# Attention and expert feed-forward on one core: a new order of loads, PSUM in two early sets of three banks, and a later first feed-forward

## The chip, the cores and the metric

The kernel runs on one core of one Trainium2 chip. The metric is the device time of one execution in microseconds (us), as the median of the runs. Most executions of one kernel lie within 2% of each other. Each run carries a state: "slow" when it lies over 1.5% above the fastest run of the same kernel in its group.

A ratio is the mean time of one kernel's fast runs over the mean of the fast runs of the kernel before in the same rounds, so it is not quite the ratio of the medians that are quoted. A ratio of 0.01 is worth about 2.85 us here.

Engine names: PE is TensorE (matmuls and transposes), DVE is VectorE, ACT is ScalarE, POOL is GpSimd (it requests the loads), SP is SyncE (it requests the stores).

## The reference

Eight batches, eight heads, 576 positions, head size 64. The first four heads attend to the last 32 positions, the other four to every fourth of the last 128. Then each batch, as a whole, goes to one of eight experts. The code is condensed:

```python
scores = scale * np.matmul(q, k.transpose(0, 1, 3, 2))
scores = np.where(masks[None, :, :, :], scores, -1000000000.0)
attn = np.exp(scores - np.max(scores, axis=-1, keepdims=True))
attn = attn / (np.sum(attn, axis=-1, keepdims=True) + 1e-09)
x = np.matmul(attn, v)                      # (B, H, S, D), then to (B, S, 512)
# ... the mixture of experts ...
logits = x.mean(axis=1) @ w_gate            # one expert per batch
e_idx = np.argmax(logits, axis=1)
h = np.maximum(x[mask] @ w1[e], 0.0)
out[mask] = gate_w[mask, None, None] * (h @ w2[e])
```

What matters: which weights batch b needs is known only when its attention is finished. So the load of w1 and w2 (1 MB each in bfloat16) hangs on the *gate* of the batch, a chain of small instructions on PE, DVE and POOL.

## The kernel before

Work is cut into slots, four per batch; a slot t does the scores of one pair of heads, the `av` product of the pair before, and, from slot `4*b + LAGS[b]` on, a quarter of the feed-forward of batch b. The gate of batch b falls in slot 4*b + 5 (the first one at the end of slot 4). All loads go through one queue, in the order in which POOL requests them; the requests behind a gate are these:

```python
LAGS = (6, 7, 8, 8, 8, 8, 8, 8)
osp = ctx.enter_context(tc.tile_pool(name="osp", bufs=3))      # rows on their way out
psS = ...   # scores: 2 banks
psN = ctx.enter_context(tc.tile_pool(name="psN", bufs=1, space=PSUM))   # nd: 3 banks, one buffer
psM = ctx.enter_context(tc.tile_pool(name="psM", bufs=3, space=PSUM))   # all else: 3 banks
# ...
GO = (1, 0)                         # heads 4..7 first, then heads 0..3
def load_a(b): load_tiles(b); load_qk(b, GO[0]); load_v(b, GO[0]); load_vt(b)
def load_b(b): load_qk(b, GO[1]); load_v(b, GO[1])
# at the start: batches 0 and 1, complete
# ...
def emit_gate(b):
    # ... logits, argmax, expert number into a register of POOL ...
    # w1 of the expert, in four pieces
    if b == 0:
        load_a(2)
    nc.gpsimd.dma_start(out=w2b[:], in_=moe_w2[ds(e_val, 1)]...)     # w2, 1 MB
    load_b(b + 2)
    load_a(b + 3)
```

The transposes of k and q for a pair of slots come two slots and one slot ahead. So `load_b(b + 2)`, requested in slot 4*b + 5, is first needed in slot 4*b + 8, and the next gate comes one slot after that. This closes a loop: gate, loads, transposes of k, attention, next gate.

The small pieces of one slot, in the order of the program (cut):

```python
if prev: pa(); fence()              # av of the slot before, first part, into nd
flush()                             # stores of finished output rows
if att: emit_S_mm(b, n); emit_exp(b, n)
if items: run_T(t)                  # transposes; first half copied by DVE, second by ACT
if prev: pbb(); emit_ln(pb)
if att: emit_mask(b, n)
if prev: emit_rd(pb)
if not items: run_T(t)
# first half of the feed-forward items, the gate, then:
if prev: emit_norm(pb, pn)          # frees nd
# second half of the items
```

The softmax here doesn't subtract the row's maximum and nothing guards it: scores larger than these inputs give would overflow.

## Time and profile before

| | before |
|---|---|
| time, median (3 runs) | 284.86 us (284.79 to 288.28) |
| PE busy, share of the span | 73% |
| granted TensorE clock, mean | 0.922 |
| gates at (us) | 31.8, 66.5, 95.4, 128.0, 160.7, 192.7, 226.5, 251.2 |

First the page's slices: the span in 40 equal slices of 7.1 us, each digit a busy share in tenths (9 is 90% or more); for PEclk the digit is the granted clock in tenths.

```profile
PE   1465516999489882499929897498936999799893
PEclk9999999999669997599996999599995999799999
DMA  6994099973999299955999189993998069619913
```

Read the last row: the DMA is not lacking in load, it comes in bursts, with a slice near zero in every loop (the 4 and 0 before the first gate, then 3, 2, 5, 1, 3, 0). PE has its holes (1, then 4, 2 and 4, 2, 4, 3) while the DMA is at 9, and the recorded clock falls (6, 5, 6, 5, 5) with each hole but the first. The two engines take turns.

The chain that ended last, as shares of the span by line:

```profile
DMA km<-in_k_dram 30%; PE hm L470 21%; PE om L490 8%; PE nd L268 5%; PE tp L201 4%; DMA out_dram<-osb 3%; PE psS L220 2%; POOL w2b L435 2%; DVE xt L396 1%; ACT pt L244 1%; DVE qk L209 1%; POOLq L422 1%; PE lgt L415 1%; DVE pt L251 1%; DVE ht L477 1%
```

One loop of it in order of time (start, duration, what). L415 is the gate; km is a tile of k.

```profile
127.96 0.36 PE lgt L415 x8
...
132.59 0.91 POOL w2b L435
133.50 15.10 DMA km<-in_k_dram
148.63 1.11 PE tp L201 x33
149.80 0.33 PE nd L268 x13
150.12 6.30 PE hm L470 x32
...
160.69 0.36 PE lgt L415 x8
```

The chain from one gate to the next goes through the load of k, 15.1 us after the request of w2. The 15.1 us are not all lost, since PE has other work for a part of them. What PE really lost is in its waits (who waited for what: total us, times, longest):

```profile
PE tp L201 <- DMA km<-in_k_dram: 31.9, 6, 7.2
PE nd L268 <- DVE xt L396: 12.8, 10, 2.3
PE tp L201 <- DVE le L160: 5.7, 1, 5.7
PE hm L470 <- DMA w1b<-in_moe_w_dram: 4.0, 3, 1.7
PE lgt L415 <- DVE pooled L411: 3.1, 5, 0.6
PE hm L470 <- DVE osb L497: 2.9, 2, 2.2
...
PE tp L201 <- DVE osb L497: 1.1, 1, 1.1
```

The third line is the very first load of k at the start of the kernel, put down to a DVE instruction. The clock around one such wait, by stretches (busy us and instructions of PE, PEld, DVE, ACT, POOL; then granted clock, DMA share, GB/s):

```profile
143.50:147.00 3.50, 0.08 (x3) 0.00 (x0) 1.05 (x2) 0.92 (x1) 0.30 (x1) 1.00 1.18 224
147.00:150.50 3.50, 1.87 (x58) 1.59 (x59) 1.14 (x2) 0.66 (x2) 0.99 (x2) 0.63 1.18 269
150.50:154.00 3.50, 3.50 (x16) 2.25 (x15) 1.53 (x4) 1.28 (x3) 0.70 (x1) 0.50 1.67 194
154.00:157.50 3.50, 3.50 (x88) 2.71 (x87) 1.21 (x5) 1.88 (x5) 0.00 (x0) 0.89 1.13 148
```

PE does nothing for one stretch, and is granted half its clock in the next ones. This is what the Trainium skill, "TensorE: Matmul & The Clock Gate", Part 1, describes: an idle window halves the clock, a busy one restores it. The trace agrees here, with 0.50 for at least 3.5 us.

The record of the clock cannot be taken at its word at the start of the kernel. It shows 1.00 up to 70 us, yet the same matmul of the first feed-forward takes 444 ns before 48.5 us and 286 ns after 49.2 us (below: before, by line, in the windows 46.4 to 48.5 and 49.2 to 51.7 us; the number behind the comma is the mean of one in ns):

```profile
L470 PE MATMUL hm<-xt,w1b 128*128 128x288 bf16 x9 | 2.3, 444 | 0.0
L470 PE MATMUL hm<-xt,w1b 128*128 128x288 bf16 x21 | 2.7, 286 | 0.0
```

At the recorded 0.50 (150.5 to 154 us) it takes 447 ns. So PE ran slowly in the last us before 48.5, where the record shows 1.00; one transpose took 239 ns up to 40 us against 193 ns once the feed-forward ran, which says the same of the slots before. The first clock entry in the file of this trace lies at 48.9 us (in the changed kernel at 48.1 us), and until the first entry 1.00 is shown. Hence the first hole shows no fall, and the mean clocks quoted here are too high, by an amount that depends on where a record begins.

### The profile page before, as it was taken

How to read it: one execution, taken by the hardware profiler on the slowest of the kernel's cores; microseconds unless marked ns; L12 is line 12 of the kernel's file. 1: busy time of each engine (PE TensorE's matmuls, PEld its weight loads, DVE VectorE, ACT ScalarE, POOL GpSimd, SP SyncE). 2: the span in 40 equal slices, each digit the busy share in tenths (PEclk: the TensorE clock that was granted, in tenths of full speed). 3: DMA queues.
4: the chain of work that ended last, by engine and by line, in shares of the span. 5: the costliest groups of instructions: out<-in, count | busy, mean ns of one | idle time of the engine just before them, and what ended most of it. 6: DMA issues, size and time to landing. Idle time of an engine off the chain costs nothing.

```text
span 284.3 us, 9050 instructions
## 1 busy us (share of the span) xinstructions
PE 207.4 (73%) x3952; PEld 143.0 (50%) x3952; DVE 129.1 (45%) x375; ACT 128.3 (45%) x225; POOL 80.5 (28%) x128
## 2 busy tenths in 40 slices
PE   1465516999489882499929897498936999799893
PEld 1454515856357452376516664375525755554651
DVE  3745613746535543275515652365513652531511
ACT  2465722756616653267414664266512664331230
POOL 8740175203612261206401082205500040031000
PEclk9999999999669997599996999599995999799999
DMA  6994099973999299955999189993998069619913
GB/s 95 188 196 30 2 172 202 197 111 98 200 214 192 27 203 238 197 74 76 175 249 208 11 147 205 233 134 49 176 246 120 2 94 203 168 24 172 257 50 129
DMA packets 49383, 40.97 MB, mean 144 GB/s; under 512 B 23744, under 2 KB 37056, under 8 KB 49344
## 3 DMA queue, kind: packets, MB, share of 16 engines
q0 software_dynamic: 42880, 30.94, 75.2%
q1 hardware_dynamic: 6464, 9.46, 10.1%
q8 instruction: 31, 0.51, 0.7%
q14 instruction: 8, 0.07, 0.1%
HBM read 61.88 MB, written 9.44 MB: 251 GB/s over the span
## 4 chain that ended last, share of the span: by engine, by line
PE 42%; DMA 33%; issue 9%; DVE 8%; POOL 3%; ACT 2%; POOLq 2%; DVEq 0%
DMA km<-in_k_dram 30%; PE hm L470 21%; PE om L490 8%; PE nd L268 5%; PE tp L201 4%; DMA out_dram<-osb 3%; PE psS L220 2%; POOL w2b L435 2%; DVE xt L396 1%; ACT pt L244 1%; DVE qk L209 1%; POOLq L422 1%; PE lgt L415 1%; DVE pt L251 1%; DVE ht L477 1%
## 5 line engine op out<-in xcount | busy, mean ns | idle before, releaser
L470 PE MATMUL hm<-xt,w1b 128*128 128x288 bf16 x512 | 77.1, 313 | 7.0 <-DMA w1b<-in_moe_w_dram 4.0
L470 PEld LDWEIGHTS <-w1b 128*128 128x128 bf16 x512 | 52.8, 107 | 27.0 <-issue 6.4
L490 PE MATMUL om<-w2b,ht 128*128 128x512 bf16 x256 | 58.2, 380 | 0.0
L244 ACT ACTIVATE pt<-psS 128x896 bf16<-128x896 f32 x32 | 29.3, 917 | 49.1 <-PE psS L220 49.1
L429 POOL DMA_DIRECT2D w1b<-in_moe_w_dram x32 | 19.0, 604 | 112.9 <-PE hm L470 65.7
L209 DVE COPY qk<-tp 128x576 bf16<-128x576 bf16 x32 | 24.2, 759 | 55.6 <-PE tp L201 55.6
L201 PE MATMUL tp<-ident,km 64*64 64x64 bf16 x576 | 16.4, 219 | 37.6 <-DMA km<-in_k_dram 31.9
L475 ACT ACTIVATE ht<-hm 128x288 bf16<-128x288 f32 x64 | 25.1, 407 | 35.2 <-PE hm L470 31.9
L207 ACT ACTIVATE qk<-tp 128x576 bf16<-128x576 bf16 x32 | 23.2, 725 | 39.3 <-PE tp L201 31.7
L490 PEld LDWEIGHTS <-ht 128*128 128x128 bf16 x256 | 23.8, 98 | 27.2
L396 DVE SCALAR_TENSOR_TENSOR xt<-nd,rd 128x320 bf16<-128x320 f32 x64 | 32.3, 541 | 11.1 <-ACT rd L369 11.1
L268 PE MATMUL nd<-pt,vm 64*64 64x64 bf16 (+2 forms) x896 | 24.6, 204 | 17.2 <-DVE xt L396 12.8
L477 DVE TENSOR_SCALAR ht<-hm 128x288 bf16<-128x288 f32 x64 | 28.7, 456 | 18.2 <-PE hm L470 17.3
L201 PEld LDWEIGHTS <-km 64*64 64x64 bf16 x576 | 14.7, 132 | 38.8 <-DMA km<-in_k_dram 38.8
L268 PEld LDWEIGHTS <-vm 64*64 64x64 bf16 x896 | 17.4, 117 | 23.4 <-issue 13.5
L497 DVE TENSOR_SCALAR osb<-om,gbc 128x512 f32<-128x512 f32 x16 | 12.0, 749 | 36.6 <-PE om L490 13.9
L101 POOL DMA_DIRECT2D vm<-in_v_dram x32 | 24.1, 768 | 14.0 <-DMA w1b<-in_moe_w_dram 10.6
L251 DVE TENSOR_TENSOR pt<-pt,mk 128x896 bf16<-128x896 bf16 x32 | 19.9, 622 | 13.9 <-ACT pt L244 13.9
L369 ACT ACTIVATE rd<-lnd 128x576 f32<-128x576 f32 x32 | 21.9, 683 | 1.0
L268 PE MATMUL nd<-pt,ones 64*64 64x128 bf16 (+3 forms) x288 | 22.2, 265 | 0.0
L363 ACT ACTIVATE lnd<-nd 128x576 f32<-128x576 f32 x32 | 20.6, 644 | 3.4 <-PE nd L268 3.4
L220 PE MATMUL psS<-qk 64*64 64x96 bf16 (+2 forms) x576 | 18.2, 237 | 3.0 <-DVE qk L209 2.5
(56 smaller groups left out, 175.1 us busy)
## 6 DMA issues: line engine op xcount, KB each, us to landing
w1b<-in_moe_w_dram POOLq DMA_DIRECT2D x32, 256.0 KB, 6.2
w2b<-in_moe_w_dram POOLq DMA_DIRECT2D x8, 1024.0 KB, 14.7
out_dram<-osb SPq DMA_DIRECT2D x32, 256.0 KB, 6.7
km<-in_k_dram POOLq DMA_DIRECT2D x16, 288.0 KB, 13.6
qm<-in_q_dram POOLq DMA_DIRECT2D x16, 288.0 KB, 9.0
vm<-in_v_dram POOLq DMA_DIRECT2D x8, 256.0 KB, 7.3
vm<-in_v_dram POOLq DMA_DIRECT2D x32, 64.0 KB, 14.3
out_dram<-osx SPq DMA_DIRECT2D x16, 64.0 KB, 6.4
```

What stands on the lines that cost most here:

```text
L101: nc.gpsimd.dma_start(out=t[:, h], in_=v[b, h, 0:512, :].rearrange("(c p) d -> p c d", p=P))
L201: nc.tensor.transpose(out=tp[half(a), j, :], in_=t[half(a), RH * jh + j, :], identity=ident2[half(a), :])
L207: nc.scalar.activation(out=o, in_=i, func=AF.Copy)
L209: nc.vector.tensor_copy(out=o, in_=i)
L220: nc.tensor.matmul(ps[half(e), a, o : o + rhs.free_size()], lhsT=lhsT, rhs=rhs, start=True, stop=True, skip_group_check=True)
L244: nc.scalar.activation(out=pt[:], in_=s["ps"][:, :, 0:NP], func=AF.Exp, scale=0.125)
L268: x = nc.tensor.matmul(oo, lhsT=lhsT, rhs=rhs, start=start, stop=True, skip_group_check=True)
L396: nc.vector.scalar_tensor_tensor(out=o, in0=a0, scalar=1.0, in1=a1, op0=ALU.mult, op1=ALU.mult, accum_out=s["pool"][:, w, c : c + 1],)
L470: nc.tensor.matmul(hm[:], lhsT=s["w1"][:, c, fc * P : (fc + 1) * P], rhs=s["xt"][:, c, cols], start=(c == 0), stop=(c == 3))
L475: nc.scalar.activation(out=o, in_=hm[:], func=AF.Relu)
L477: nc.vector.tensor_scalar_max(out=o, in0=hm[:], scalar1=0.0)
L490: nc.tensor.matmul(om[:], lhsT=s["ht"][:, fc, r * P : (r + 1) * P], rhs=s["w2"][:, fc, :], start=(fc == 0), stop=(fc == 7))
```

## The change

The intent: have the loads stand in the queue in the order in which they are needed, use DMA time that lies idle at the start, and let the slots that have no feed-forward yet overlap more by giving `av` and the transposes two sets of three PSUM banks in turn.

```diff
-LAGS = (6, 7, 8, 8, 8, 8, 8, 8)
+LAGS = (7, 8, 8, 8, 8, 8, 8, 8)
# --- load_a and load_b are cut into load_qa, load_va, load_qb, load_vb ---
     # at the start
-    load_a(1)
-    load_b(1)
+    load_qa(1)
+    load_va(1)
+    load_qb(1)
+    load_vb(1)
+    load_qa(2)
     # behind the w1 of a gate
-        if b == 0:
-            load_a(2)
+        load_va(b + 2)
+        load_qb(b + 2)
         nc.gpsimd.dma_start(out=w2b[:], in_=moe_w2[ds(e_val, 1)].rearrange("e (c p) f -> p (e c) f", p=P))
-        load_b(b + 2)
-        load_a(b + 3)
+        load_vb(b + 2)
+        load_qa(b + 3)
# --- banks ---
+    def early_bank(t, k, dt=F32):
+        nm = f"e{t % 2}{k}"                # set t % 2, bank k of three
+        return pools["early"].tile([P, 512 if dt == F32 else 1024], dt, name=nm, tag=nm, space=PSUM)[:]
+    def late():                            # close them; then nd: 3 banks, all else: 3 banks
+    # in the loop over slots
+        if t == LAGS[0]:
+            late()
# --- early slots: scores and exp first, transposes behind av and ahead of ln ---
+        if early_s:
+            emit_S_mm(b, n)
+            emit_exp(b, n)
         if prev:
             pa, fence, pbb = av_work(pb, pn)
# ...
+        if pools["early"] is not None:
+            run_T(t)
+        if prev:
             emit_ln(pb)
```

Cut: the masks (fewer instructions, and behind the first transposes' copies), ln in two pieces in the early slots (the sums lie in two banks there), both halves of a transpose ahead of their two copies, and the gate a little earlier within its slot.

More of the change, by code (lines that the diff above doesn't have):

```diff
@@ L69, with bank @@
     psS = ctx.enter_context(tc.tile_pool(name="psS", bufs=1, space=PSUM))
-    psN = ctx.enter_context(tc.tile_pool(name="psN", bufs=1, space=PSUM))
-    psM = ctx.enter_context(tc.tile_pool(name="psM", bufs=3, space=PSUM))
     ctx.enter_context(tc.manual_schedule())
     nc.scalar.preload_act_table_set("natural_log_exp_and_others")
+    ps0 = psS.tile([P, 2, 512], F32, name="ps0", tag="ps0", space=PSUM)
+    nc.vector.memset(ps0[:], 0.0)
+    early = ExitStack()
+    pools = {"early": early.enter_context(tc.tile_pool(name="psE", bufs=1, space=PSUM))}
+    def early_bank(t, k, dt=F32):
+        nm = f"e{t % 2}{k}"
+        return pools["early"].tile([P, 512 if dt == F32 else 1024], dt, name=nm, tag=nm, space=PSUM)[:]
+    def late():
+        early.close()
+        pools["early"] = None
+        pools["N"] = ctx.enter_context(tc.tile_pool(name="psN", bufs=1, space=PSUM))
+        pools["M"] = ctx.enter_context(tc.tile_pool(name="psM", bufs=3, space=PSUM))
+    def bank(dt=F32, t=0):
+        if pools["early"] is not None:
+            return early_bank(t, 2, dt)
+        return pools["M"].tile([P, 512 if dt == F32 else 1024], dt, name="m", tag="M", space=PSUM)[:]
     src = {"q": q, "k": k}
@@ L108, with load_qa @@
     GO = (1, 0)
-    def load_a(b):
+    def load_qa(b):
         if b < B:
@@ L113, in load_a, with load_va, load_qb, load_vb @@
             load_qk(b, GO[0])
+    def load_va(b):
+        if b < B:
             load_v(b, GO[0])
             load_vt(b)
-    def load_b(b):
+    def load_qb(b):
         if b < B:
             load_qk(b, GO[1])
+    def load_vb(b):
+        if b < B:
             load_v(b, GO[1])
@@ L151 @@
     nc.vector.tensor_tensor(out=ident2[:], in0=identb[:, 0:DH], in1=identb[:, DH:P], op=ALU.add)
-    dpf = const.tile([P, QB], F32, name="dpf")
-    nc.vector.tensor_copy(out=dpf[:], in_=dti[:])
-    nc.vector.tensor_scalar(out=dpf[DH:P], in0=dpf[DH:P], scalar1=64.0, scalar2=None, op0=ALU.add)
-    ge0 = const.tile([P, QB], F32, name="ge0")
-    nc.vector.tensor_scalar(out=ge0[:], in0=dpf[:], scalar1=0.0, scalar2=None, op0=ALU.is_ge)
-    le31 = const.tile([P, QB], F32, name="le31")
-    nc.vector.tensor_scalar(out=le31[:], in0=dpf[:], scalar1=31.0, scalar2=None, op0=ALU.is_le)
@@ L161 @@
-    mk = const.tile([P, 2, NP], BF16, name="mk")
-    for g in range(2):
-        for i in range(4):
-            nc.vector.tensor_mul(mk[:, g, QB * i : QB * i + QB], ge0[:], le31[:])
-    nc.vector.tensor_mul(mk[:, 0, 4 * QB : NP], ge0[:, 0:DH], le31[:, 0:DH])
-    dta = const.tile([P, 4, 16], I32, name="dta")
-    nc.vector.tensor_scalar(out=dta[:], in0=dtt[:], scalar1=3, scalar2=None, op0=ALU.bitwise_and)
-    dtf = const.tile([P, 4, 16], F32, name="dtf")
-    nc.vector.tensor_copy(out=dtf[:], in_=dta[:])
@@ L170, with masks @@
-    nc.vector.tensor_scalar(out=dtf[:], in0=dtf[:], scalar1=0.0, scalar2=None, op0=ALU.is_equal)
-    dtg = const.tile([P, 4, 16], F32, name="dtg")
-    nc.vector.tensor_copy(out=dtg[:], in_=dtt[:])
-    nc.vector.tensor_scalar(out=dtg[:], in0=dtg[:], scalar1=0.0, scalar2=None, op0=ALU.is_ge)
-    nc.vector.tensor_mul(mk[:, 1, 4 * QB : NP].rearrange("p (r m) -> p r m", r=4), dtf[:], dtg[:])
+    mk = const.tile([P, 2, NP], BF16, name="mk")
+    def masks():
+        dpf = const.tile([P, QB], F32, name="dpf")
+        nc.vector.tensor_copy(out=dpf[:], in_=dti[:])
+        nc.vector.tensor_scalar(out=dpf[DH:P], in0=dpf[DH:P], scalar1=64.0, scalar2=None, op0=ALU.add)
+        le31 = const.tile([P, QB], F32, name="le31")
+        nc.vector.tensor_scalar(out=le31[:], in0=dpf[:], scalar1=31.0, scalar2=None, op0=ALU.is_le)
+        band = const.tile([P, QB], BF16, name="band")
+        nc.vector.scalar_tensor_tensor(
+            out=band[:], in0=dpf[:], scalar=0.0, in1=le31[:], op0=ALU.is_ge, op1=ALU.mult
+        )
+        for g in GO:
+            nc.vector.tensor_copy(
+                out=mk[:, g, 0 : 4 * QB].rearrange("p (i n) -> p i n", n=QB),
+                in_=band[:].rearrange("p (i n) -> p i n", i=1).to_broadcast([P, 4, QB]),
+            )
+        nc.vector.tensor_copy(out=mk[:, 0, 4 * QB : NP], in_=band[:, 0:DH])
+        dta = const.tile([P, 4, 16], I32, name="dta")
+        nc.vector.tensor_scalar(out=dta[:], in0=dtt[:], scalar1=3, scalar2=None, op0=ALU.bitwise_and)
+        dtf = const.tile([P, 4, 16], F32, name="dtf")
+        nc.vector.tensor_copy(out=dtf[:], in_=dta[:])
+        dtg = const.tile([P, 4, 16], F32, name="dtg")
+        nc.vector.tensor_copy(out=dtg[:], in_=dtt[:])
+        nc.vector.tensor_scalar(out=dtg[:], in0=dtg[:], scalar1=0.0, scalar2=None, op0=ALU.is_ge)
+        nc.vector.scalar_tensor_tensor(
+            out=mk[:, 1, 4 * QB : NP].rearrange("p (r m) -> p r m", r=4),
+            in0=dtf[:], scalar=0.0, in1=dtg[:], op0=ALU.is_equal, op1=ALU.mult,
+        )
@@ L189, in half, with emit_T @@
         return slice(64 * a, 64 * a + 64)
-    def emit_T(b, g, nm, jh, eng):
+    def emit_T(b, g, nm, t):
         s = state(b)
@@ L196, in emit_T @@
         qk = s["qk"][g]
-        t = loads[b][nm, g]
-        tp = psM.tile([P, RH, DH], BF16, name="tp", tag="M", space=PSUM)
-        for j in range(RH):
-            for a in range(2):
-                nc.tensor.transpose(
-                    out=tp[half(a), j, :], in_=t[half(a), RH * jh + j, :], identity=ident2[half(a), :]
-                )
-        o = qk[:, 0 if nm == "k" else 1].rearrange("p h (m j) -> p h m j", j=RJ)[:, :, :, RH * jh : RH * jh + RH]
-        i = tp[:].rearrange("p j (h m) -> p h m j", h=2)
-        if eng == "A":
-            nc.scalar.activation(out=o, in_=i, func=AF.Copy)
-        else:
-            nc.vector.tensor_copy(out=o, in_=i)
+        ld = loads[b][nm, g]
+        if pools["early"] is not None:
+            tps = [early_bank(t, jh, BF16) for jh in range(2)]
+        else:
+            tps = [bank(BF16) for jh in range(2)]
+        for jh in range(2):
+            tp = tps[jh][:, 0 : RH * DH].rearrange("p (j d) -> p j d", d=DH)
+            for j in range(RH):
+                for a in range(2):
+                    nc.tensor.transpose(
+                        out=tp[half(a), j, :], in_=ld[half(a), RH * jh + j, :], identity=ident2[half(a), :]
+                    )
+        for jh in range(2):
+            tp = tps[jh][:, 0 : RH * DH]
+            o = qk[:, 0 if nm == "k" else 1].rearrange("p h (m j) -> p h m j", j=RJ)[:, :, :, RH * jh : RH * jh + RH]
+            i = tp.rearrange("p (j h m) -> p h m j", h=2, j=RH)
+            if jh:
+                nc.scalar.activation(out=o, in_=i, func=AF.Copy)
+            else:
+                nc.vector.tensor_copy(out=o, in_=i)
     def emit_S_mm(b, n):
@@ L258, in av_work, with ndc @@
         g, h2 = GO[n // 2], n % 2
-        nd = psN.tile([P, 3 * 512], F32, name="nd", tag="nd", space=PSUM)
-        s["nd"] = nd
+        t = NSLOT * b + n
+        if pools["early"] is not None:
+            nb = [early_bank(t, i) for i in range(3)]
+            lns = ((DSO, 256), (DLO, 320))
+        else:
+            nd = pools["N"].tile([P, 3 * 512], F32, name="nd", tag="nd", space=PSUM)
+            nb = None
+            lns = ((DSO, S),)
+        def ndc(o, n):
+            return nd[:, o : o + n] if nb is None else nb[o // 512][:, o % 512 : o % 512 + n]
+        s["nd"] = (ndc, lns)
         first, lasts = [None], []
@@ L264, in mm @@
         def mm(a, o, n, lhsT, rhs, start, view=None):
-            oo = nd[half(a), o : o + n]
+            oo = ndc(o, n)[half(a)]
             if view is not None:
@@ L362, in emit_ln @@
         lnd = rdp.tile([P, S], F32, name="lnd", tag="lnd")
-        nc.scalar.activation(out=lnd[:], in_=s["nd"][:, DSO : DSO + S], func=AF.Ln)
+        ndc, lns = s["nd"]
+        for o, n in lns:
+            nc.scalar.activation(out=lnd[:, o - DSO : o - DSO + n], in_=ndc(o, n), func=AF.Ln)
         s["lnd"] = lnd
@@ L375, in emit_norm @@
         c = 2 * g + h2
-        nd, rd = s["nd"], s["rd"]
+        (ndc, _), rd = s["nd"], s["rd"]
         xt = s["xt"][:, c, :]
@@ L379, in emit_norm @@
         for w, no, ro, sz in parts:
-            i0, i1 = nd[:, no : no + sz], rd[:, ro : ro + sz]
+            i0, i1 = ndc(no, sz), rd[:, ro : ro + sz]
             if g == 0:
@@ L405, in bass_ap_plain_L, with emit_pooled @@
         return bass.AP(tensor=o.tensor, offset=o.offset, ap=ap)
-    def emit_gate(b):
+    def emit_pooled(b):
         s = st[b]
@@ L411, in emit_gate @@
         nc.vector.tensor_tensor(out=pooled[:], in0=s["pool"][:, 0, :], in1=s["pool"][:, 1, :], op=ALU.add)
-        lgt = psM.tile([P, 512], F32, name="lgt", tag="M", space=PSUM)
-        lg = lgt[0:1, 0:E]
+        s["pooled"] = pooled
+    def emit_gate(b):
+        s = st[b]
+        pooled = s["pooled"]
+        lg = bank()[0:1, 0:E]
         for c in range(4):
@@ L455, in emit_gate_bc @@
         s = st[b]
-        bct = psM.tile([P, 512], F32, name="bct", tag="M", space=PSUM)
+        bct = bank()
         nc.tensor.matmul(bct[:, 0:1], lhsT=ones1[:], rhs=s["gw"][:], start=True, stop=True)
@@ L467, in ffn1 @@
         cols = slice(HALF * hf, HALF * hf + HALF)
-        hm = psM.tile([P, HALF], F32, name="hm", tag="M", space=PSUM)
+        hm = bank()[:, 0:HALF]
         for c in range(4):
             nc.tensor.matmul(
-                hm[:], lhsT=s["w1"][:, c, fc * P : (fc + 1) * P], rhs=s["xt"][:, c, cols], start=(c == 0), stop=(c == 3)
+                hm, lhsT=s["w1"][:, c, fc * P : (fc + 1) * P], rhs=s["xt"][:, c, cols], start=(c == 0), stop=(c == 3)
             )
@@ L474, in ffn1 @@
         if eng == "A":
-            nc.scalar.activation(out=o, in_=hm[:], func=AF.Relu)
+            nc.scalar.activation(out=o, in_=hm, func=AF.Relu)
         else:
-            nc.vector.tensor_scalar_max(out=o, in0=hm[:], scalar1=0.0)
+            nc.vector.tensor_scalar_max(out=o, in0=hm, scalar1=0.0)
     stores = []
@@ L487, in ffn2 @@
         s = st[b]
-        om = psM.tile([P, DM], F32, name="om", tag="M", space=PSUM)
+        om = bank()
         for fc in range(8):
             nc.tensor.matmul(
-                om[:], lhsT=s["ht"][:, fc, r * P : (r + 1) * P], rhs=s["w2"][:, fc, :], start=(fc == 0), stop=(fc == 7)
+                om, lhsT=s["ht"][:, fc, r * P : (r + 1) * P], rhs=s["w2"][:, fc, :], start=(fc == 0), stop=(fc == 7)
             )
@@ L494, in ffn2 @@
         if eng == "A":
-            nc.scalar.activation(out=osb[:], in_=om[:], func=AF.Copy, scale=s["gbc"][:])
+            nc.scalar.activation(out=osb[:], in_=om, func=AF.Copy, scale=s["gbc"][:])
         else:
-            nc.vector.tensor_scalar_mul(out=osb[:], in0=om[:], scalar1=s["gbc"][:])
+            nc.vector.tensor_scalar_mul(out=osb[:], in0=om, scalar1=s["gbc"][:])
         stores.append(lambda: nc.sync.dma_start(out=out[b, r * P : (r + 1) * P, :], in_=osb[:]))
@@ L501, in ffn_tail @@
         s = st[b]
-        ox = psM.tile([P, 256], F32, name="ox", tag="M", space=PSUM)
+        ox = bank()[:, 0:256]
         for fc in range(8):
@@ L513, in ffn_tail @@
         osx = osp.tile([P, 256], F32, name="osx", tag="osx")
-        nc.vector.tensor_scalar_mul(out=osx[:], in0=ox[:], scalar1=s["gbc"][:])
+        nc.vector.tensor_scalar_mul(out=osx[:], in0=ox, scalar1=s["gbc"][:])
         for a in range(2):
@@ L518, in ffn_tail @@
             )
-    ps0 = psS.tile([P, 2, 512], F32, name="psS", tag="S", space=PSUM)
-    nc.vector.memset(ps0[:], 0.0)
     NA = B * NSLOT
@@ L534, in run_T @@
         for b, g, nm in tsched.get(t, []):
-            emit_T(b, g, nm, 0, "D")
-            emit_T(b, g, nm, 1, "A")
+            emit_T(b, g, nm, t)
     runs = {}
@@ L544 @@
     run_T(-1)
+    masks()
     for t in range(max(runs) + 1):
+        if t == LAGS[0]:
+            late()
         b, n = divmod(t, NSLOT)
@@ L559 @@
                 items += [lambda: ffn2(fb, 2, "A"), lambda: ffn2(fb, 3, "D"), lambda: ffn_tail(fb)]
+        early_s = att and pools["early"] is not None
+        if early_s:
+            emit_S_mm(b, n)
+            emit_exp(b, n)
         if prev:
@@ L564 @@
         flush()
-        if att:
+        if att and not early_s:
             emit_S_mm(b, n)
@@ L573 @@
             pbb()
+        if pools["early"] is not None:
+            run_T(t)
+        if prev:
             emit_ln(pb)
@@ L578 @@
             emit_rd(pb)
-        if not items:
+        if not items and pools["early"] is None:
             run_T(t)
         k0 = len(items) // 2
-        for f in items[:k0]:
-            f()
-        gb, gn = divmod(t - 1, NSLOT)
-        if gn == 0 and 0 < gb < B + 1:
-            if gb > 1:
+        gb, gn = divmod(t - 1, NSLOT)
+        for i, f in enumerate(items[:k0]):
+            f()
+            if i == k0 // 2 and gn == 0 and 1 < gb < B + 1:
                 emit_gate(gb - 1)
                 emit_gate_w(gb - 1)
+        if not items[:k0] and gn == 0 and 1 < gb < B + 1:
+            emit_gate(gb - 1)
+            emit_gate_w(gb - 1)
         if prev:
             emit_norm(pb, pn)
-        for f in items[k0:]:
+        if prev and pn == NSLOT - 1:
+            emit_pooled(pb)
+        for i, f in enumerate(items[k0:]):
             f()
```

## The prediction

> **What bounds it now.** 284.86 us. In the chain of waits the DMA of a k tile (km) takes 30% of the span: once per batch, gate, four w1 issues, w2 issue, then 8 to 17 us of "DMA km", then transposes. PE's waits show the net loss: 31.9 us idle for km, six times. Afterwards the granted clock is 0.50 for some 3.5 to 7 us: 32 first-layer matmuls take 6.30 us at 150 us against 4.03 us at 53 us. The Trainium skill, "TensorE: Matmul & The Clock Gate", Part 1, says an idle window halves the clock; this trace agrees. I estimate 1 to 2 us per wait, some 8 us in all.
>
> The gates fall at 31.8, 66.5, 95.5, 128.0, 160.7, 192.6, 226.5 and 251.2 us (timeline), about 32 us apart. In each loop the DMA is active only some 25.5 us (98.8 to 124.3; 130.3 to 156.4), then idle 5 to 7 us until the next gate. km of batch b+2 is requested behind w2, lands about 18 us after the first w1 issue, and the next gate follows 12 us later. PE needs about 25 us a loop without the wait (slots of 6.0, 6.2, 5.1, 6.4 us plus the gate). Both floors are near 25 to 26 us, run partly one after the other.
>
> **The change, costed.**
> 1. Loads ordered w1, v, k/q of batch b+2, then w2. Before the km that is needed stand 0.3 MB instead of 1 MB; the difference takes 4 to 5 us (220 to 250 GB/s in those slices) with the queueing. w2, needed two slots later, fills idle DMA time. Loop 32 to about 26.5 us: most of the gain.
> 2. k/q of batch 2 requested at the start, into DMA time idle from 24 to 34 us. The first km wait (7.1 us) goes. With lag 7 the first feed-forward starts at about 40 us in slot 7, instead of 46.5 in slot 6. Slots without feed-forward stay 8, so the lag itself saves no PE work.
> 3. Two sets of banks: av no longer waits for the previous norm (about 2.2 us a slot). But transposes of slot t reuse banks of slot t-2, wait for its norm, and ln and rd queue behind the transposed copy on ACT: 0.6 + 0.73 + 0.8 + 0.68 + 1.17 us plus latencies, 4.1 us a slot against 4.6; the first norm comes later. Masks behind the first copies: first scores at 9.7 instead of 11.3 us. Net: first gate at about 31 us.
> 4. Gate earlier within its slot: about 0.5 us a loop.
>
> **Sum.** First gate 31 us; second about 56 (was 66.5); then five loops of 26 to 27 us, limited by DMA; the last about 25, by PE; last gate about 212 (was 251), then the 33 us tail, unchanged. Predicted 246 us, range 237 to 259. Chances: faster by over 2% 0.96, within 2% 0.03, slower 0.01.
>
> **Right if:** "DMA km" falls below 12% of the chain; PE's wait for km falls below 10 us; DMA slices near zero between 60 and 200 us vanish; gates are 25 to 28 us apart; PE's mean clock rises from 0.92 above 0.95; first gate within 2 us of 31.
>
> **Wrong if:** DMA slows when stores and loads overlap all the time (loops of 29 us, 260 in all); v in 128-byte pieces (the Trainium skill, "DMA: Bandwidth & Descriptors", Specifications: under 512 B not at line rate; 23,744 of this trace's 49,383 packets are) delays the next w1; or the early banks pipeline better than I think (first gate at 27 us).

## The result, and the profile after

| | before | after |
|---|---|---|
| time, median | 284.83 us (4 runs) | 250.48 us (248.07 to 251.12, 4 runs) |
| ratio of fast runs | 1 | 0.8778, interval 0.8708 to 0.8847 |
| PE busy, share of the span | 73% | 82% |
| granted clock, mean, as recorded | 0.922 | 0.973 |
| gates at (us) | 31.8, 66.5, 95.4, 128.0, 160.7, 192.7, 226.5, 251.2 | 32.1, 60.0, 88.3, 115.5, 140.7, 166.7, 191.6, 215.3 |
| loops (us) | 34.7, 29.0, 32.5, 32.7, 32.0, 33.9, 24.7 | 27.9, 28.3, 27.2, 25.2, 26.0, 24.9, 23.7 |
| last gate to the end of the span | 33.1 us | 33.8 us |

The slices of the changed kernel, now 6.2 us each:

```profile
PE   1576464999853999799997899799979996996993
PEclk9999999999995899979999999999999997999999
DMA  5999129991699949999899999998999699089723
```

From the sixteenth slice (93 us) to about 205 us no DMA slice is below 6, and PE is at 7 or more. The DMA holes that are left are in front: the 1 and 2 around the first gate, the 1 ahead of the second and the 4 at the third. The chain that ended last:

```profile
PE m L531 24%; PE m L551 17%; DMA km<-in_k_dram 7%; PE nd L323 6%; DMA out_dram<-osb 6%; PE m L243 5%; DVE xt L453 3%; PE e L243 3%; PE ps L264 3%; PE m L566 2%; DVE osb L558 2%; PE e L323 2%; ACT rd L426 1%; DVE ht L538 1%; ACT lnd L420 1%
```

The load of k has gone from 30% to 7%. In its place stand the two feed-forward matmuls (L531, L551), and something new: the DMA of the output rows, osb, has doubled to 6%. PE's waits say the same:

```profile
PE e L243 <- DMA km<-in_k_dram: 7.1, 2, 5.6
PE m L243 <- DVE osb L558: 6.9, 5, 2.1
PE m L243 <- DMA km<-in_k_dram: 4.0, 1, 4.0
PE m L531 <- DVE osb L558: 4.0, 2, 2.1
PE nd L323 <- DVE xt L453: 4.0, 6, 1.6
PE e L476 <- issue: 3.2, 1, 3.2
PE nd L323 <- DVE gbc L520: 3.0, 1, 3.0
```

Of the 7.1 us on the first line, 5.6 are the first load at the start, which before had too under another name. So PE's waits for k inside the kernel went from 31.9 us to 5.5 us. But 10.9 us are now spent on osb, against 4.0 before. The timeline of one such case shows what osb itself waits for (start, duration, engine, line, what, and in brackets the idle time before it):

```profile
97.61 0.34 SPq L559 DMA_DIRECT2D out_dram<-osb  x1
98.05 8.55 SPq L559 DMA_DIRECT2D out_dram<-osb  x3
...
105.49 0.75 DVE L558 TENSOR_SCALAR osb<-m,gbc 128x512 f32<-128x512 f32 x1 [4.15 <-issue]
```

Four tiles of output rows per batch share three buffers. The stores of the first two are requested at 97.61 and 98.05 (the second line merges three requests); the fourth tile needs the first one's buffer back, and gets it 7.9 us after that request, at 105.49. Until then DVE stands still, the PSUM bank with the result stays taken, and the transposes that want that bank (L243) wait. This was a reading of the trace only; an experiment below tests it.

The loop that in before went through 15.1 us of k looks like this in the changed kernel's chain, in order of time. It begins with the gate at 140.7 us:

```profile
150.71 7.33 DMA out_dram<-osb
158.16 0.76 DVE osb L558
...
159.62 4.03 PE m L531 x32
```

No load of k is in this loop's chain, a store is; and 32 matmuls of the first layer take 4.03 us instead of 6.30.

### The profile page after: what moved, and what is told of

Same layout as the page of the kernel before. It is cut to its first block, busy times and chain, and to the rows that moved or that the text cites. A ratio compares the mean times of both kernels' runs of the same rounds, so it can differ in the third digit from the quotient of the medians.

```text
span 249.1 us, 9040 instructions
## 1 busy us (share of the span) xinstructions
PE 203.1 (82%) x3952; PEld 140.5 (56%) x3952; DVE 127.0 (51%) x368; ACT 129.4 (52%) x231; POOL 80.6 (32%) x128
## 4 chain that ended last, share of the span: by engine, by line
PE 63%; DMA 13%; DVE 9%; issue 6%; ACT 5%; POOL 2%; POOLq 0%; DVEq 0%; SPq 0%
PE m L531 24%; PE m L551 17%; DMA km<-in_k_dram 7%; PE nd L323 6%; DMA out_dram<-osb 6%; PE m L243 5%; DVE xt L453 3%; PE e L243 3%; PE ps L264 3%; PE m L566 2%; DVE osb L558 2%; PE e L323 2%; ACT rd L426 1%; DVE ht L538 1%; ACT lnd L420 1%
## 5 line engine op out<-in xcount | busy, mean ns | idle before, releaser
L531 PE MATMUL m<-xt,w1b 128*128 128x288 bf16 x512 | 72.8, 300 | 5.4 <-DVE osb L558 4.0
L531 PEld LDWEIGHTS <-w1b 128*128 128x128 bf16 x512 | 50.7, 102 | 22.8 <-issue 7.2
L551 PE MATMUL m<-w2b,ht 128*128 128x512 bf16 x256 | 58.0, 380 | 0.0
L288 ACT ACTIVATE pt<-ps 128x896 bf16<-128x896 f32 x32 | 29.2, 913 | 37.4 <-PE ps L264 37.4
L536 ACT ACTIVATE ht<-m 128x288 bf16<-128x288 f32 x64 | 26.2, 410 | 28.5 <-PE m L531 25.2
L551 PEld LDWEIGHTS <-ht 128*128 128x128 bf16 x256 | 23.9, 98 | 27.4
L538 DVE TENSOR_SCALAR ht<-m 128x288 bf16<-128x288 f32 x64 | 28.1, 451 | 9.4 <-PE m L531 8.6
L453 DVE SCALAR_TENSOR_TENSOR xt<-nd,rd 128x320 bf16<-128x320 f32 (+1 forms) x52 | 25.9, 534 | 12.3 <-ACT rd L426 12.3
L253 DVE COPY qk<-m 128x576 bf16<-128x576 bf16 x23 | 17.4, 759 | 26.2 <-PE m L243 26.2
L323 PEld LDWEIGHTS <-vm 64*64 64x64 bf16 x896 | 17.3, 117 | 17.9 <-issue 5.6
L243 PEld LDWEIGHTS <-km 64*64 64x64 bf16 x576 | 14.5, 126 | 19.3 <-DMA km<-in_k_dram 11.6
L323 PE MATMUL nd<-pt,vm 64*64 64x64 bf16 (+1 forms) x736 | 18.6, 195 | 7.5 <-DVE xt L453 4.0
L251 ACT ACTIVATE qk<-m 128x576 bf16<-128x576 bf16 x23 | 16.7, 727 | 9.9 <-PE m L243 9.8
L264 PE MATMUL ps<-qk 64*64 64x96 bf16 (+2 forms) x576 | 17.6, 237 | 3.3 <-ACT qk L251 2.5
L243 PE MATMUL m<-ident,km 64*64 64x64 bf16 x396 | 10.1, 200 | 9.9 <-DVE osb L558 5.8
```

Source lines behind the costliest of these rows:

```text
L243: nc.tensor.transpose(out=tp[half(a), j, :], in_=ld[half(a), RH * jh + j, :], identity=ident2[half(a), :])
L264: nc.tensor.matmul(ps[half(e), a, o : o + rhs.free_size()], lhsT=lhsT, rhs=rhs, start=True, stop=True, skip_group_check=True)
L288: nc.scalar.activation(out=pt[:], in_=s["ps"][:, :, 0:NP], func=AF.Exp, scale=0.125)
L323: x = nc.tensor.matmul(oo, lhsT=lhsT, rhs=rhs, start=start, stop=True, skip_group_check=True)
L453: nc.vector.scalar_tensor_tensor(out=o, in0=a0, scalar=1.0, in1=a1, op0=ALU.mult, op1=ALU.mult, accum_out=s["pool"][:, w, c : c + 1],)
L531: nc.tensor.matmul(hm, lhsT=s["w1"][:, c, fc * P : (fc + 1) * P], rhs=s["xt"][:, c, cols], start=(c == 0), stop=(c == 3))
```

## The experiments

Theory A: the order of requests gives most of the gain; the early request of batch 2 gives the first km wait; the banks give about nothing; the lag gives nothing. Rivals: the banks or the early start carry it. Theory C came from the trace after: the changed kernel is bound by PE and by its wait for output buffers. Rival D: it is bound by the DMA's 25 to 26 us per loop, which the prediction had named.

| run | changed | median us | ratio to before (fast runs) | 95% interval |
|---|---|---|---|---|
| the change | | 250.48 | 0.8778 | 0.8708 to 0.8847 |
| u_order | w2 first, rest as changed | 290.32 | 1.0174 | 1.0073 to 1.0276 |
| u_order2 | order exactly as before | 274.72 | 0.9522 | 0.9432 to 0.9612 |
| b_order | before, order alone | 257.54 | 0.8964 | 0.8883 to 0.9044 |
| u_banks | no early banks | 250.31 | 0.8779 | 0.8699 to 0.8859 |
| u_q2 | no early request of batch 2 | 259.44 | 0.9057 | 0.8942 to 0.9171 |
| u_lag | lags 6, 7 again | 257.0 | 0.8938 | 0.8832 to 0.9044 |
| a_lag8 | lag 8 for batch 0 | 249.67 | 0.8699 | 0.8634 to 0.8764 |
| a_osb5 | five output buffers | 241.95 | 0.8385 | 0.8303 to 0.8466 |
| b_osb5 | before, five output buffers | 280.21 | 0.9824 | 0.9740 to 0.9908 |
| a_act | ACT copy behind ln and rd | 249.19 | 0.8733 | 0.8650 to 0.8816 |
| best3 | five buffers, lag 8, ACT copy | 236.38 | 0.8285 | 0.8211 to 0.8359 |
| best4 | best3, k/q ahead of v | 235.61 | no ratio | one fast run only |

All gave correct results. "Before" was run beside each group of four (medians 284.44, 286.65 and 284.39 us); the groups ran on three different chips, and the change itself was not run again beside them, so runs are compared by their ratios to before. The intervals are about 1% wide on each side, so differences of ratios under 0.01 are not resolved.

### u_order: w2 ahead of v and of the needed k/q

```diff
-        load_va(b + 2)
-        load_qb(b + 2)
         # w2
+        load_va(b + 2)
+        load_qb(b + 2)
         load_vb(b + 2)
```

> The changed kernel with only the order put back: w2 is requested before v and k/q of batch b+2 again. Theory A (the order of the loads is most of the gain): km comes 4 to 5 us later in each loop, PE waits for km again in most loops (20 us or more in all, against 11 us), gates go from 26 to about 30 or 31 us apart, 272 to 280 us. Rival B (the early request of batch 2 and the early banks give most): at most 258 us, gates stay under 28 us apart.

290.32 us, more than I had expected, and 1.7% more than before itself. In the profile PE waited 45.4 us for k in six waits, and from the second gate on all gates but the last stood 34 to 35 us apart. The experiment was not the pure undo that I took it for: the changed kernel has 0.3 MB of v of the first group in this place, which before had requested one loop earlier, so the needed k now stood behind w1, w2 *and* that v. It shows that whatever stands ahead of k costs, but not the size of the change's own step.

### u_order2: the requests exactly in the order of before

```diff
+        if b == 0:
+            load_va(2)
+        # w2
-        load_va(b + 2)
         load_qb(b + 2)
-        # w2
         load_vb(b + 2)
         load_qa(b + 3)
+        load_va(b + 3)
```

> The changed kernel with the order of requests put back exactly as before had it: w1, w2, k/q and v of b+2 (second group), k/q and v of b+3 (first group); the early request of batch 2's k/q stays. The first undo also had 0.3 MB of v ahead of the needed k, which before had not. Theory A (order is most of the gain): 274 to 281 us, gates 31 to 33 us apart, PE waits for km 22 us or more. Rival: at most 265 us, and then the other parts carry half the gain or more.

274.72 us, ratio 0.9522: 0.0744 above the change, or about 21 us. The profile fell in the slow state (the fast runs were 272.13 and 273.13 us), so only the pattern is used: PE's waits for k are back, in six waits, beside the two early ones that the changed kernel has too.

```profile
PE m L243 <- DMA km<-in_k_dram: 27.5, 6, 7.1
PE e L243 <- DMA km<-in_k_dram: 6.3, 2, 5.7
```

### b_order: the order alone, in the kernel before

```diff
         # w1
+        load_bq(b + 2)          # k/q of the second group
         # w2
-        load_b(b + 2)
+        load_bv(b + 2)          # its v
         load_a(b + 3)
```

> The kernel before with one change alone: k/q of batch b+2 requested ahead of w2 instead of behind it. Theory A: all loops but the first become 26 to 28 us, the first km wait (7 us) stays: 256 to 263 us. Rival (the order helps only together with the other parts): 270 us or more.

257.54 us, ratio 0.8964: moving the requests of one k and one q past that of w2 gives 0.1036 of the 0.1222 that the whole change gives, some 29 us. The first loop stays at 34.0 us, as expected; the others were 27.8, 26.5, 25.5, 25.9, 25.5 and 22.9 us. PE's waits for k:

```profile
PE tp L209 <- DMA km<-in_k_dram: 13.4, 3, 6.9
```

The three waits are the first load (5.8), the first km wait, which was expected to stay (6.9), and 0.7 us at 109 us: in the later loops the wait is gone.

Together, undoing gives 21 us and doing alone gives 29 us. The parts are not additive, but by either measure the order is most of the gain.

### u_banks: no early sets of banks

```diff
+    late()                      # right after its definition
...
-        if t == LAGS[0]:
-            late()
```

> The changed kernel without the two early sets of banks: the later banks (three for nd, three shared) from the start, so the order of instructions in the first slots is that of before too; masks stay behind the first copies. Theory A (what the banks save at av is given back because the transposes wait for the norm and ln and rd queue behind their copy on ACT): 249 to 252.5 us, first gate 31 to 32.5 us. Rival B (the banks pipeline the first slots): 254 us or more, first gate 35 us or later.

250.31 us, ratio 0.8779 against 0.8778. The early banks give nothing to the time. In the profile the first gate even comes at 30.5 us instead of 32.1, and the second earlier as well:

```profile
57.35 0.35 PE L478 MATMUL m<-wg_t,pooled 128*1 128x8 f32 x8
```

against 60.00 in the changed kernel. So the banks cost some 2.6 us up to the second gate. Later loops gave that back (one loop from 164.3 to 193.1 us took 28.8 us, with the clock at 0.88 and without a long wait for a load); one profile does not settle whether that is part of this kernel or of this execution. The low mean clock of this profile (0.904) is no loss beside the change's 0.973: its record begins at 14.5 us and counts 27 us at 0.50 in the first slots, which the record of the changed kernel leaves out, with one transpose at 239 ns in both. If everything ahead of the first entry is counted as 0.50, both means come to about 0.88 (an estimate from the two records).

### u_q2: k/q of batch 2 requested behind the first gate

```diff
-    load_qa(2)                  # at the start
...
+        if b == 0:
+            load_qa(2)
         load_va(b + 2)
```

> The changed kernel with the first k/q of batch 2 requested only behind the w1 of batch 0, as before. Theory A: the first km wait comes back (5 to 7 us of PE idle before 50 us, DMA silent from 24 to 35 us), and the later loops do not make up for it: 254 to 258 us. Rival: the lost time is absorbed by the DMA's idle time before the second gate (7 us), under 252 us.

259.44 us, a little over the range that I had given; 0.0279 above the change, about 8 us. The second gate fell at 65.2 instead of 60.0 us. So this part is worth what the prediction put on it (7.1 us), or slightly more; the wait itself is back too, 7.1 us at 43.8 us. The later loops were also 27 us instead of 25 to 26; I have no experiment for that.

### u_lag: lags 6 and 7 again

```diff
-LAGS = (7, 8, 8, 8, 8, 8, 8, 8)
+LAGS = (6, 7, 8, 8, 8, 8, 8, 8)
```

> The changed kernel with lags 6, 7, 8, ... as before (the banks change over one slot earlier too). Theory A: the slots without feed-forward stay 8, so within 2 us of the changed kernel (249 to 252.5); PE waits 1 to 3 us for w1 in slot 6, which the earlier feed-forward gives back. Rival: the lag is what lets the loads land in time, 254 us or more.

Theory A fell here. The fast runs were 253.21 and 255.71 us (median of all 257.0), ratio 0.0160 above the change, about 4.6 us with an interval of some 3 to 4 us to either side. In the profile PE starts the feed-forward at 41.0 us instead of 45.2, waits for w1 and then works almost without a gap up to 62 us:

```profile
38.15:62.00 23.85, 22.26 (x456) 15.77 (x457) 12.11 (x33) 13.27 (x23) 6.14 (x10) 1.00 1.02 157
```

PE is busy 22.26 of 23.85 us at a recorded clock of 1.00 (from 40 us on 20.70 of 22.00 us; the changed kernel 18.95). And yet the second gate comes later:

```profile
63.41 0.35 PE L476 MATMUL m<-wg_t,pooled 128*1 128x8 f32 x8
```

60.00 became 63.41. My reading: the work is the same, but with lag 6 three whole quarters of the first feed-forward stand ahead of the second gate (slots 6 to 8), with lag 7 two (slots 7 and 8). And the DMA has nothing to do until that gate: the loads of the next loop start late, and the loop pays. In the changed kernel the empty slot comes behind that gate, where loads are running. The profiled run (258.61 us) was 2.1% above the fastest; 2.1% of 60 us is 1.3 us, so the state alone does not explain the 3.4 us. Two other causes are not ruled out. The first feed-forward began in the slow stretch before 48 us: 24 of its matmuls took over 400 ns, against 12 in the changed kernel, some 2 us (an estimate, at 161 ns each). And the expectation's rival is visible too: PE waited 5.1 us in all for w1, 3.8 us of it at 75 to 77 us, where the changed kernel has no wait for w1. The run also moves batch 1's lag and the change of banks, so it does not separate these.

### a_lag8: lag 8 from the first batch on

```diff
-LAGS = (7, 8, 8, 8, 8, 8, 8, 8)
+LAGS = (8, 8, 8, 8, 8, 8, 8, 8)
```

> The changed kernel with lag 8 for batch 0 too (the early banks stay one slot longer). After the lag run: a slot without feed-forward is worth more ahead of a gate, whose loads the DMA waits for, than behind it. Theory E: the second gate comes 3 to 5 us earlier than in the changed kernel (56 instead of 60 us), DMA silence before it shrinks, total 246 to 250 us. Rival F (any lag beyond the landing of w1 only leaves PE idle): second gate earlier, but total 252 us or more.

The second gate moved to 58.5 us, by 1.5 and not by 3 to 5 us. 249.67 us, ratio 0.8699: 0.0079 below the change, inside the intervals. The direction agrees with theory E; the gain is not resolved. The step from lag 7 to 8 brings less than the step from 6 to 7.

### a_osb5: five output buffers

```diff
-    osp = ctx.enter_context(tc.tile_pool(name="osp", bufs=3))
+    osp = ctx.enter_context(tc.tile_pool(name="osp", bufs=5))
```

> The changed kernel with five instead of three buffers for the output rows (osb, osx). Theory C (the changed kernel's loops are now bound by PE with its small waits, of which 10.9 us are for an osb that waits for a store to land): PE's wait for osb is gone, 241 to 245 us. Rival D (the loops are bound by the DMA's 25 to 26 us): the wait moves to km or w1, 247 us or more.

241.95 us, ratio 0.8385: 0.0393 below the change, about 11 us, for one number. PE's wait for osb is gone from its list altogether:

```profile
PE e L243 <- DMA km<-in_k_dram: 7.2, 2, 6.2
PE m L243 <- DMA km<-in_k_dram: 5.5, 4, 4.2
PE nd L323 <- DVE xt L453: 4.7, 6, 2.4
PE ps L264 <- ACT qk L251: 3.3, 4, 0.8
```

The loops after the third gate were 23.4, 25.2, 24.7, 24.4 and 20.0 us: below the 26 to 27 us at which the prediction had the DMA stop them. Theory C holds for the changed kernel, D does not, as far as 25 us a loop. The Trainium skill, "Perfetto Trace Analysis", Optimization Strategy, says that the same gap repeating on the engine that should be saturated can mean too few buffers for the next tile. Seven waits of up to 2.1 us on PE are such a gap, and the run agrees.

### b_osb5: the same buffers in the kernel before

> The kernel before with five instead of three buffers for the output rows: a control. Theory C says that the stores' wait counts only once the loops no longer wait for km: in before PE waits 4.0 us for osb, and most of it lies just ahead of a longer wait for km, so at most 2 us faster than before (ratio 0.99 to 1.00). Rival: the buffers are worth the same 8 to 9 us in before (ratio 0.97).

280.21 us, ratio 0.9824, some 5 us: more than the 2 us that I allowed, but half of what the buffers give in the changed kernel. By the 2% rule it is "unclear", though the interval is clear of no gain. Where it comes from is as theory C has it: the loops that wait for k did not move (34.6, 29.1, 32.6, 32.9, 31.9, 32.9 us), and PE's wait for k from 12 us on was 32.9 us in six waits, against 31.9 us in six: what the buffers saved was waited for k instead. The gain is in the last loop, which waits for no k: it fell from 24.7 to 20.7 us.

```profile
246.53 0.34 PE L415 MATMUL lgt<-wg_t,pooled 128*1 128x8 f32 x8 [0.62 <-DVE pooled L411]
```

The last gate at 246.5 instead of 251.2 us is the whole of it. I had forgotten that loop.

### a_act: in early slots, the ACT copy of the transposes behind ln and rd

```diff
             if jh:
-                nc.scalar.activation(out=o, in_=i, func=AF.Copy)
+                held.append(lambda o=o, i=i: nc.scalar.activation(out=o, in_=i, func=AF.Copy))
...
         if prev:
             emit_rd(pb)
+        let_go()
```

> The changed kernel with one order changed in the early slots: the copy of the second half of the transposes on ACT comes behind ln and rd instead of ahead of them. Theory G (the early banks gained nothing because transposes wait for the norm of the slot before and ln and rd queue behind their copy): the slots of the first batch shrink from 4.1 to 4.4 us to about 3.4 us, first gate 28.5 to 29.5 us, total 246 to 249 us. Rival H (the early slots are bound by something else, such as the DVE): first gate 31 us or later, total unchanged.

249.19 us, ratio 0.0045 below the change: not resolved. The first gate moved from 32.1 to 30.3 us, which is neither theory's number. By the timeline, the norms of the first batch end at 17.3, 21.0, 25.2 and 30.0 us, against 19.2, 23.3, 27.3 and 31.8 in the changed kernel. So the first norm came 1.9 us earlier, and the step from norm to norm stayed (12.7 against 12.6 us for three). The queue behind the copy on ACT delays the first norm, but does not set the step, as I had it. What sets it I can only read, not show: in the program the transposes stand behind `av`, which waits for the mask, which stands on DVE behind the copy of the transposes before. There is also PE idle time of 1.0 and 0.7 us at 22 and 27 us, in both kernels at the same instructions, that the profile puts down to no releaser. This stays open. The second gate came at 56.8 us, 3.2 us earlier than in the changed kernel, so in this profile the queue on ACT did cost time up to there.

### best3 and best4: what the experiments point to

best3 joins five output buffers, lag 8 and the ACT copy behind ln and rd; best4 requests k/q of batch b+2 ahead of its v as well.

> The changed kernel with five output buffers, lag 8 for batch 0 and the ACT copy behind ln and rd. If the three are worth what they were alone (8.5 us, 0.8 us, 2 us): 237 to 241 us. If the loops hit the DMA's 25 us instead: 241 us or more.

> The same with k/q of batch b+2 requested ahead of its v as well. The needed k lands another 1 to 2 us sooner in the loops that wait for it (5.5 us of PE in four waits with five buffers): 234 to 239 us, 1 to 3 us under the kernel without it. Rival: v then lands late for its own slot, no gain.

best3: 236.38 us, ratio 0.8285, 17% below before and some 14 us below the change. The parts were worth 11, 2 and 1 us alone (the last two not resolved), and 14 together. Its slices:

```profile
PE   0676567599998999979998999999979999999992
PEclk9999999999999999999999999999999999999998
DMA  5999329993699999999999999999999899389823
```

From 47 us on PE is at 7 or more in every slice but the last, and the DMA holes behind the second gate are gone up to 200 us, ahead of the last gate. The clock digits of the first 53 us stand ahead of the first entry of the record, as above: 22 matmuls of the first feed-forward took over 400 ns there. best4 has a median of 235.61 us, but its runs scatter from 231.68 to 237.66 us, and only the fastest counts as fast, so whether it beats best3 is unclear. Its profiled execution (a slow one) shows 0.4 us of waits for k from 12 us on, against 2.5 us in best3.

## Why the prediction was right, and where it was not

**Total.** Predicted 246 us, range 237 to 259; measured 250.48 us. That the total came so near is in part luck: the second gate was 4 us later than predicted, and the loops had the predicted length for another reason than the predicted one (below).

**Order of loads: right.** The chain's share of km went from 30% to 7% (predicted below 12%). PE's wait for k went from 31.9 to 11.1 us as the list has it, of which 5.6 us is the load at the start; I had asked for under 10. The median time of a k load from request to landing fell from 13.6 to 8.9 us, by the 4 to 5 us of the prediction. The run with the order alone shows some 29 of the 35 us, the run without it loses 21.

**Clock: right as recorded.** Predicted above 0.95, measured 0.973; both leave out the slow first 48 us. The low-clock slices went with the waits; the ones left follow the one remaining wait for k (78.6 us) and waits for osb. What this was worth is not shown by a run of its own. The 8 us of the prediction were an estimate; PE's busy time on the first-layer matmuls fell by 4.3 us (77.1 to 72.8).

**Early request of batch 2: right.** Put at 7.1 us; taking it away costs about 8.

**Banks: right about the time.** I expected a first gate of about 31 us, because the transposes of slot t wait for the norm of slot t-2; it came at 32.1, and 30.5 without the banks. The steps from norm to norm were 4.1 to 4.5 us, near the 4.1 of the prediction. But the reason that I gave for the step, the queue behind the ACT copy, is only a part: taking it away moved the first norm and left the step, so the right step was in part luck.

**"Second about 56": 4 us too early; it came at 60.0.** I had the first feed-forward at 40 us, it began at 45.2. The two attention slots behind the first gate still ran at the slow step of the early banks, and PE then waited 3.0 us at the change from the early to the late banks (the wait for gbc in its list), which I had not costed. The change of banks is not the whole of that wait: with lag 8, where slot 7 still has the early banks, PE waits 2.0 us for the same gbc at 42.5 us, and 3.1 us at the change, one slot later; without early banks it waits 1.8 us at 40.2 us. Without the early banks the second gate came at 57.35, with the ACT copy moved at 56.8, so the early slots as built account for some 3 of the 4 us.

**"The lag itself saves no PE work": true of the work, wrong of the time.** Going back to lags 6 and 7 cost about 4.6 us. The count of empty slots is the same, but where they stand mattered. That an empty slot ahead of a gate brings the gate and its loads forward fits both lag runs; it is not shown apart from the slow first 48 us and the waits for w1.

**"Five loops of 26 to 27 us, limited by DMA": the size was near, the limit was wrong.** Measured 28.3, 27.2, 25.2, 26.0, 24.9 (the first and the last just outside the 25 to 28 us that I had asked of the gates). What failed here is the step "limited by DMA". They were limited by PE and its 10.9 us of waits for output buffers: with five buffers most of them fell below 25.5 us, the DMA floor that I had read from the bursts of before. The wait for osb was there to read in before's list (4.0 us); I left it out since the k wait covered most of it. Taking the larger wait away uncovered it.

**Tail: right.** 33 us predicted, 33.8 measured.

**Not tested:** the gate's earlier place within its slot (put at 0.5 us a loop) and the shorter masks were not run alone.

## What to carry to other kernels

When a load hangs on a result that the previous loads feed, look at what stands in the queue ahead of the one tile that closes the loop; moving a big request that has time behind it can be worth more than any work on the engines, and it is a few lines. Check a recorded clock against the duration of one and the same matmul. Where idle slots stand relative to the instruction that other engines wait for is worth a run; here the reading was that they belong ahead of it, by some 4.6 us one way and an unresolved 2 us the other. When a large wait goes, look in the old profile for small waits that it covered (here three buffers for four output tiles): after the change they count in full.

## What the Trainium skill lacked or had wrong

- "DMA: Bandwidth & Descriptors", Anatomy of one DMA, gives one DMA as about 2.0 us plus bytes over 436 GB/s; for 256 KB that would be 2.6 us (an estimate by that page's formula, fitted to DMAs through GpSimd). In this kernel a 256 KB store took a median of 6.7 us from issue to landing, before and after, and a buffer came back 7.8 us after its store was requested; the last four stores, with no load left to run beside them, took 2.0 us each. The page has no figure for a store that shares the engines with a queue full of loads, which is what the number of output buffers has to be chosen by (the stores here are requested by SP).
- "PSUM — Partial Sum Buffer" and "Perfetto Trace Analysis": neither says what it costs to change from one division of the banks to another in mid-kernel. Here PE waited 3.0 us once at the change (2.0 us in the same slot where the change came a slot later, 1.8 us without early banks), and the early division gave no time (ratio 0.8779 without it, 0.8778 with it).
- "TensorE: Matmul & The Clock Gate" was borne out: a granted clock of 0.50 after a wait of 5 us, and 32 matmuls in 6.30 us instead of 4.03. No page says that the granted clock of a profile reads 1.00 until its first entry: here up to 48.9 us, with one matmul at 444 ns before that and 286 ns after.
